# Order of DVE's work in the V stage: the fourth SwiGLU unit's products ahead of the statistics of tiles 10 and 11

## The chip, the cores and the metric

The kernel runs on one core of a Trainium2 chip. The metric is the device time of one execution in microseconds (us); the time of a kernel is the median of several executions. The engines are called PE (TensorE, matmuls), DVE (VectorE), ACT (ScalarE), POOL (GpSimd) and SP (SyncE, which here issues the DMAs). Each engine works through its own list of instructions in order, and waits where an instruction needs what another engine or a DMA has not yet finished.

## The reference

With x of 2048 tokens by 640 features (bf16), the kernel computes the sum of x, a linear attention and a SwiGLU block, both of them on the same layer norm of x:

```python
xn  = layernorm(x)                              # over 640 features, eps 1e-5
# A: linear attention with the hedgehog feature map, 32 heads of 20
q, k, v = split_heads(xn @ wqkv)
pq, pk  = q @ w_phi, k @ w_phi                  # per head, 20 x 20
phi_q = concat(softmax(pq), softmax(-pq));  phi_k = concat(softmax(pk), softmax(-pk))
kv = phi_k^T @ v;   z = sum over tokens of phi_k
A  = merge_heads((phi_q @ kv) / (phi_q . z + 1e-6)) @ wo
# B: SwiGLU with 1536 hidden features
B  = (silu(xn @ w1) * (xn @ w3)) @ w2
out = x + A + B
```

## The kernel before, in words

The 2048 tokens are 16 tiles of 128. The order of all instructions is written out by hand (`manual_schedule`): what stands earlier in the source stands earlier in the list of its engine, and the framework adds the waits and hands out the buffers. The stages are: an opening with the layer norm of the first tiles; the V stage, in which all tiles are normalized and transposed and V is computed; a stage over 16 tiles for phi_k and kv; and a stage over 16 tiles for phi_q, the quotient and the output. SwiGLU units are put in between as filling for PE.

In the V stage the steps of a tile t are these.

- `stats(t0, n)`: `ln_stats` on DVE for each tile (two BATCH_NORM_STATS2, L205, and an aggregate, L208), then on POOL, for the n tiles together, `ln_pow` (L216, L219) and `ln_newton` (L233 to L244), which make the reciprocal standard deviation `rstd`. For tiles 12 and 13 POOL adds `shift` (L246).
- `lx(t0, n)`: x is normalized in place, on DVE (L259), or for tiles 12 and 13 on ACT (L254), with `rstd` and the mean (or `shift`).
- `T(t, ...)`: the tile's transpose into `xnT`, for t of 4 and up a transposing DMA on SP's queue (L269). On the same queue, in the order written, stand `ldT` (L122), which loads blocks of the key and query weights transposed, and the plain loads (L109).
- `V(t)`: ten matmuls on PE into two PSUM banks (L295), and three copies by ACT into `vaug` (L308).
- `FB(d)`: the key weights' block d is multiplied by w_phi on PE (L377) with the masked weights `wphi`, which DVE makes once in `phi_blocks()` (L368), and ACT copies it into `wkphi` (L386).

A SwiGLU unit is split in two. `unit()` puts ten matmuls on PE (gate `gp` and up `up`, L393, one PSUM bank each) and the tanh on ACT (L401) where it stands. It returns a function, and where this is called (`g0()` to `g5()`), DVE does the products: L406 (from tanh and gate, which frees the gate's bank) and L409 (times up, which frees the up bank). So the source says apart when PE does a unit and when DVE does its products.

`V`, the units and later steps take their PSUM banks from one pool of six (`bank`); which bank a step gets depends on which were given back before it in the source.

The stage's end, after the lines of the change, is

```python
        V(9)
        g5 = unit()
        lx(13, 1)
        T(13)
        ldT(wkT, 1, 3)
        V(10)
        phi_blocks()
        g5()
        lx(14, 2)
        T(14, 15)
        ldT(wkT, 1, 4)
        V(11)
        ld_glu(512, F)
        ...
        V(12), FB(0), FB(1), V(13), FB(2), V(14), FB(3), V(15), FB(4)
```

Of the kernel before, what the change touches and what calls it, by code (L numbers as in the profile page):

```python
# [12 lines left out]
def kernel(  # L13
# [105 lines left out]
    with tc.manual_schedule():  # L119
# [81 lines left out]
        def ln_stats(t, between=None):  # L201
            xt = xin[:, (t // 4) % 3, t % 4, :]
            st = work.tile([P, 2, 6], f32, name="st")
            for i in range(2):
                nc.vector.bn_stats(out=st[:, i, :], in_=xt[:, i * HD : (i + 1) * HD])  # L205
                if i == 0 and between:
                    between()
            nc.vector.bn_aggr(out=mv[:, t, :], in_=st[:])  # L208
# [5 lines left out]
        def ln_pow(t, n):  # L214
            r = slice(t, t + n)
            nc.gpsimd.tensor_scalar(  # L216
                out=ve[:, r], in0=mv[:, r, 1], scalar1=EPS, scalar2=None, op0=ALU.add
            )
            nc.gpsimd.tensor_tensor(out=ry[:, r], in0=ve[:, r], in1=mhalf[:, 0:n], op=ALU.pow)  # L219
# [8 lines left out]
        def ln_newton(t, n):  # L228

            r = slice(t, t + n)  # L230
            eng = nc.gpsimd
            if n == 1:
                eng.tensor_scalar(  # L233
                    out=rstd[:, r], in0=ry[:, r], scalar1=ve[:, r], scalar2=ry[:, r],
                    op0=ALU.mult, op1=ALU.mult,
                )
            else:
                eng.tensor_mul(out=rstd[:, r], in0=ry[:, r], in1=ry[:, r])
                eng.tensor_mul(out=rstd[:, r], in0=rstd[:, r], in1=ve[:, r])
            eng.tensor_scalar(  # L240
                out=rstd[:, r], in0=rstd[:, r], scalar1=-0.5, scalar2=1.5,
                op0=ALU.mult, op1=ALU.add,
            )
            eng.tensor_mul(out=rstd[:, r], in0=rstd[:, r], in1=ry[:, r])  # L244
            if t in BY_ACT:
                eng.tensor_scalar(  # L246
                    out=shift[:, r], in0=mv[:, r, 0], scalar1=rstd[:, r], scalar2=-1.0,
                    op0=ALU.mult, op1=ALU.mult,
                )
# [138 lines left out]
        def glu_unit(sc, fi):  # L388

            gp, up = bank("gp"), bank("up")  # L390
            for ps, w in ((gp, w1), (up, w3)):
                for c in range(KD):
                    nc.tensor.matmul(  # L393
                        ps[:],
                        w[:, c, fi * P : (fi + 1) * P],
                        xnT[:, c, sc * 512 : (sc + 1) * 512],
                        start=(c == 0),
                        stop=(c == KD - 1),
                    )
            th = work.tile([P, 512], f32, name="th")  # L400
            nc.scalar.activation(out=th[:], in_=gp[:], func=AF.Tanh, scale=0.5)  # L401
            return lambda: glu_product(sc, fi, gp, up, th)
# [175 lines left out]
        def stats(t0, n):  # L578
            for t in range(t0, t0 + n):
                ln_stats(t)  # L580
            ln_pow(t0, n)
            ln_newton(t0, n)

        def lx(t0, n):
            if t0 < BY_DMA:
                nc.vector.reciprocal(out=rstd[:, t0 : t0 + n], in_=ry[:, t0 : t0 + n])
            for t in range(t0, t0 + n):
                ln_x(t)
# [13 lines left out]
        def unit():  # L602
            return glu_unit(*glu.pop(0))
# [52 lines left out]
        g3 = unit()  # L656
# [3 lines left out]
        ldT(wkT, 1, 2)  # L660
        V(4)
        V(5)
        stats(10, 2)
        g3()
        V(6)
        V(7)
        stats(12, 1)
        g4 = unit()
        lx(10, 2)
        T(10, 11)  # L670
        stats(13, 1)
        V(8)
        g4()
        stats(14, 2)
        lx(12, 1)
        T(12)
        V(9)
        g5 = unit()
        lx(13, 1)
# [123 lines left out]
```

## Time and profile before

| | |
|---|---|
| median of 3 runs | 270.49 us (270.46 to 270.83) |
| the profiled execution | 270.34 us |
| its span, first to last instruction | 268.5 us |
| granted PE clock, mean | 1.000 |
| busy: PE, DVE, ACT, POOL | 263.7, 188.7, 111.6, 95.3 us |
| 21.90 to 44.45 us: PE, DVE, ACT, POOL busy | 22.32, 13.89, 14.48, 8.91 of 22.55 us |

Times in the profile are counted from the first instruction. The stretch from 21.90 to 44.45 us is the V stage from V(4) on. A line of the timeline has the start, the length, the engine, the source line, the operation with its result and inputs, and how many like instructions are merged; in brackets, how long the engine stood idle before it and what ended that. "SPq" is the issue of a DMA on SP's queue.

### The profile page before, as it was taken

The page shows a single profiled execution, that of the slowest core. Times are in us where ns is not written, and L with a number is a line of the kernel's source. Part 1 is how long each engine was busy: PE and PEld are TensorE (multiplying, and loading weights), DVE is VectorE, ACT ScalarE, POOL GpSimd, SP SyncE. Part 2 cuts the span into 40 slices and gives each one's busy share as a digit, 9 for nine tenths or more (in the row PEclk, how much of TensorE's full clock was granted, in tenths as well). Part 3 has the DMA queues.
Part 4 walks back from the last instruction along what each step waited for, and adds up shares of the span by engine and source line. Part 5 has one row for each costly group of instructions (what it writes and reads, how often), then busy time and mean ns, then how long its engine had stood idle before and what let it go on. Part 6 is the DMA issues. An engine that isn't in the chain of part 4 may idle for free.

```text
span 268.5 us, 5276 instructions
## 1 busy us (share of the span) xinstructions
PE 263.7 (98%) x1990; PEld 166.2 (62%) x1990; DVE 188.7 (70%) x348; ACT 111.6 (42%) x342; POOL 95.3 (35%) x99
## 2 busy tenths in 40 slices
PE   8999999999999999999999999999999999999995
PEld 7646567555555555555555445677777777777773
DVE  4899940887766677777777888966766777776341
ACT  3854568544555554346556545422222222221000
POOL 5054730354433333334444321233344444433000
DMA  6996647970000000000000854345555555565831
GB/s 215 351 221 123 77 99 222 270 193 4 0 0 2 1 2 0 0 4 0 0 2 0 242 162 98 81 122 137 125 143 142 129 129 127 132 147 131 155 98 55
DMA packets 63101, 27.81 MB, mean 104 GB/s; under 512 B 50144, under 2 KB 61792, under 8 KB 63072
## 3 DMA queue, kind: packets, MB, share of 16 engines
q1 hardware_dynamic: 63072, 27.43, 42.1%
q8 instruction: 17, 0.28, 0.4%
q14 instruction: 12, 0.10, 0.1%
HBM read 12.81 MB, written 2.62 MB: 57 GB/s over the span
## 4 chain that ended last, share of the span: by engine, by line
PE 89%; DVE 4%; POOL 2%; DMA 2%; issue 1%; SPq 1%; ACT 1%; DVEq 0%
PE acc L517 28%; PE gp L393 18%; PE up L393 18%; PE pq L295 8%; PE pk L295 8%; PE pv L295 5%; PE pr L454 2%; PE pkv L419 2%; DMA reg_w<-in_A_wqkv_dram 2%; DVE st L205 1%; PE pf L377 1%; SPq L109 1%; DVE reg_h L259 1%; POOL ry L219 1%; DVE gs L406 0%
## 5 line engine op out<-in xcount | busy, mean ns | idle before, releaser
L359 POOL TENSOR_TENSOR phi<-phi,rk 128x1320 bf16<-128x1320 bf16 x32 | 77.2, 2413 | 134.1 <-DVE rk L358 99.2
L356 DVE TENSOR_REDUCE sk<-phi 128x66 f32<-128x1320 bf16 x32 | 48.9, 1528 | 41.8 <-ACT phi L322 40.8
L393 PEld LDWEIGHTS <-w 128*128 128x128 bf16 x480 | 45.5, 98 | 50.6
L393 PE MATMUL up<-xnT,w 128*128 128x512 bf16 x240 | 59.6, 379 | 0.0
L393 PE MATMUL gp<-xnT,w 128*128 128x512 bf16 x240 | 59.6, 378 | 0.0
L295 PEld LDWEIGHTS <-xnT 128*128 128x128 bf16 x480 | 45.4, 98 | 21.6 <-issue 1.0
L517 PE MATMUL acc<-reg_v,reg_h 128*128 128x320 bf16 (+2 forms) x384 | 54.9, 299 | 0.0
L322 ACT ACTIVATE phi<-pq 128x360 bf16<-128x360 f32 (+2 forms) x96 | 24.8, 364 | 58.0 <-issue 44.1
L517 PEld LDWEIGHTS <-reg_h 128*128 128x128 bf16 x384 | 37.3, 98 | 14.4
L401 ACT ACTIVATE th<-gp 128x512 f32<-128x512 f32 x48 | 28.9, 602 | 32.9 <-PE gp L393 32.9
L409 DVE SCALAR_TENSOR_TENSOR reg_h<-gs,up 128x512 bf16<-128x512 bf16 x48 | 33.0, 688 | 4.9
L322 ACT ACTIVATE phi<-pk 128x360 bf16<-128x360 f32 (+2 forms) x96 | 24.8, 364 | 24.1 <-PE pk L295 24.1
L406 DVE SCALAR_TENSOR_TENSOR gs<-th,gp 128x512 bf16<-128x512 f32 x48 | 31.5, 657 | 0.3 <-ACT th L401 0.3
L526 DVE TENSOR_TENSOR res<-acc,xr 128x320 bf16<-128x320 f32 (+2 forms) x32 | 14.3, 487 | 20.0 <-PE acc L517 20.0
L295 PE MATMUL pk<-wkphi,xnT 128*128 128x360 bf16 (+1 forms) x160 | 24.5, 299 | 0.0
L517 PE MATMUL acc<-reg_w,reg_v 128*128 128x320 bf16 (+2 forms) x160 | 24.5, 299 | 0.0
L295 PE MATMUL pq<-wqphi,xnT 128*128 128x360 bf16 (+1 forms) x160 | 24.3, 299 | 0.0
L295 PE MATMUL pv<-reg_w,xnT 128*128 128x360 bf16 (+1 forms) x160 | 23.7, 299 | 0.4 <-DVE gs L406 0.2
L358 DVE RECIPROCAL rk<-sk 128x66 f32<-128x66 f32 x32 | 18.1, 567 | 3.5 <-DVE sk L356 0.5
L517 PEld LDWEIGHTS <-reg_v 128*128 128x128 bf16 x160 | 15.7, 98 | 6.1
L308 ACT CAST reg_v<-pv 128x360 bf16<-128x360 f32 (+2 forms) x48 | 13.2, 353 | 7.7 <-PE pv L295 7.6
L205 DVE BATCH_NORM_STATS2 st<-reg_h 128x6 f32<-128x320 bf16 x32 | 13.8, 471 | 2.8 <-DMA reg_h<-in_A_x_dram 2.8
(66 smaller groups left out, 132.8 us busy)
## 6 DMA issues: line engine op xcount, KB each, us to landing
w<-in_B_w_dram SPq DMA_DIRECT2D x2, 1280.0 KB, 8.6
xr<-in_A_x_dram SPq DMA_DIRECT2D x16, 160.0 KB, 2.5
out_dram<-res SPq DMA_DIRECT2D x15, 160.0 KB, 1.8
reg_h<-in_A_x_dram SPq DMA_DIRECT2D x7, 320.0 KB, 5.4
reg_v<-in_B_w_dram SPq DMA_DIRECT2D x4, 480.0 KB, 5.4
w<-in_B_w_dram SPq DMA_DIRECT2D x4, 320.0 KB, 6.5
reg_w<-in_A_wqkv_dram SPq DMA_DIRECT2D x2, 320.0 KB, 4.2
reg_w<-in_A_wo_dram SPq DMA_DIRECT2D x1, 480.0 KB, 4.7
```

The costliest lines, as they stand in the source:

```text
L205: nc.vector.bn_stats(out=st[:, i, :], in_=xt[:, i * HD : (i + 1) * HD])
L295: nc.tensor.matmul(ps[i][:, 0 : b - a], xnT[:, c, cols], w[:, c, a:b], start=(c == 0), stop=(c == KD - 1), skip_group_check=True,)
L322: nc.scalar.activation(out=dst[:, c0 : c0 + n, g, 0:k], in_=p.rearrange("p (c f) -> p c f", c=n), func=AF.Exp, scale=1.0 - 2.0 * g,)
L356: nc.vector.reduce_sum(out=sk[:], in_=rows, axis=AX.X)
L358: nc.vector.reciprocal(out=rk[:], in_=sk[:])
L359: nc.gpsimd.tensor_mul(out=rows, in0=rows, in1=rk[:, :, :, None].to_broadcast([P, 2 * NCH, 3, Dh]))
L393: nc.tensor.matmul(ps[:], w[:, c, fi * P : (fi + 1) * P], xnT[:, c, sc * 512 : (sc + 1) * 512], start=(c == 0), stop=(c == KD - 1),)
L401: nc.scalar.activation(out=th[:], in_=gp[:], func=AF.Tanh, scale=0.5)
L406: nc.vector.scalar_tensor_tensor(out=gs[:], in0=th[:], scalar=1.0, in1=gp[:], op0=ALU.add, op1=ALU.mult)
L409: nc.vector.scalar_tensor_tensor(out=hT[:, 4 * sc : 4 * sc + 4, fi, :], in0=gs[:].rearrange("p (t s) -> p t s", t=4), scalar=0.5, in1=up[: ...
L517: nc.tensor.matmul(ps[:, 0 : b - a], rows[j][0], rows[j][1][:, a:b], start=(j == 0), stop=(j == len(rows) - 1),)
L526: nc.vector.tensor_tensor(out=res[:, a:b], in0=ps[:, 0 : b - a], in1=xr[:, a:b], op=ALU.add)
```

## The change

DVE does the fourth unit's products (`g3()`) ahead of the statistics of tiles 10 and 11. The fifth unit's products (`g4()`) come ahead of the statistics of tile 13, and those of tiles 14 and 15 come after the transpose of tile 12 is written. The statement `g4 = unit()` trades places with `stats(12, 1)`, which changes no engine's order. The instructions on PE, ACT, POOL and SP keep their order; the PSUM banks of the V steps and units from V(6) on are other ones.

```diff
         V(4)
         V(5)
+        g3()
         stats(10, 2)
-        g3()
         V(6)
         V(7)
+        g4 = unit()
         stats(12, 1)
-        g4 = unit()
         lx(10, 2)
         T(10, 11)
-        stats(13, 1)
         V(8)
         g4()
-        stats(14, 2)
+        stats(13, 1)
         lx(12, 1)
         T(12)
+        stats(14, 2)
         V(9)
         g5 = unit()
         lx(13, 1)
```

## The prediction

> **What bounds the kernel now.** I read the page first, then TensorE's gaps, then each engine's timeline from 20 to 46 us, where the moved lines run. The page's busy shares and its chain of work:
>
> ```profile
> PE 263.7 (98%) x1990; PEld 166.2 (62%) x1990; DVE 188.7 (70%) x348; ACT 111.6 (42%) x342; POOL 95.3 (35%) x99
> ...
> PE 89%; DVE 4%; POOL 2%; DMA 2%; issue 1%; SPq 1%; ACT 1%; DVEq 0%
> ```
>
> TensorE (PE) is busy 98% of the span and carries 89% of the chain, at a granted clock of 1.00 throughout. So DVE time is worth nothing by itself: an edit counts only by the time in which PE stands still. Between 21.9 and 44.45 us (the V stage after its SwiGLU opening) the timeline of PE shows one stall:
>
> ```profile
> 24.32 1.95 PE L295 MATMUL pv<-reg_w,xnT 128*128 128x360 bf16 x13
> 26.49 0.28 PE L295 MATMUL pv<-reg_w,xnT 128*128 128x280 bf16 x1 [0.23 <-DVE gs L406]
> ```
>
> This is the second matmul of V(7). Singly, its predecessor starts at 25.95 and the usual distance of such a pair is 0.15 us; here it is 0.54. The stall is therefore 0.39 us, not the 0.23 shown (ends of matmuls are modelled). The bank that V(7) takes was read by the fourth unit's first product (`g3()`, L406). DVE shows why that is late:
>
> ```profile
> 23.77 0.88 DVE L205 BATCH_NORM_STATS2 st<-reg_h 128x6 f32<-128x320 bf16 x2
> 24.69 0.21 DVE L208 BATCH_NORM_AGGREGATE mv<-st 128x2 f32<-128x12 f32 x1
> 24.81 0.83 DVE L205 BATCH_NORM_STATS2 st<-reg_h 128x6 f32<-128x320 bf16 x2
> 25.68 0.21 DVE L208 BATCH_NORM_AGGREGATE mv<-st 128x2 f32<-128x12 f32 x1
> 25.81 0.63 DVE L406 SCALAR_TENSOR_TENSOR gs<-th,gp 128x512 bf16<-128x512 f32 x1
> ```
>
> The statistics of tiles 10 and 11 stand ahead of it, though its tanh was done at 21.6. It ends at 26.44; V(7) goes on 0.05 later.
>
> Downstream of the statistics is a long line: aggregate on DVE, a chain of small operations on POOL, the normalization `lx` (DVE; ACT for tiles 12 and 13), the transposing DMA on SP's queue, then V(t) on PE. POOL for tile 13 and the start for 14 and 15, then SP:
>
> ```profile
> 30.80 0.22 POOL L216 TENSOR_SCALAR ve<-mv 128x1 f32<-128x1 f32 x1
> ...
> 32.47 0.19 POOL L244 TENSOR_TENSOR rstd<-rstd,ry 128x1 f32<-128x1 f32 x1
> 32.77 0.26 POOL L246 TENSOR_SCALAR shift<-mv,rstd 128x1 f32<-128x1 f32 x1
> 33.44 0.86 POOL L216 TENSOR_SCALAR ve<-mv 128x2 f32<-128x2 f32 x1 [0.41 <-DVE mv L208]
> ```
>
> ```profile
> 34.40 0.91 ACT L254 ACTIVATE reg_h<-reg_h,shift,rstd 128x640 bf16<-128x640 bf16 x1
> ```
>
> ```profile
> 35.34 1.20 SPq L269 DMA_TRANSPOSE xnT<-reg_h  x1
> 36.59 1.27 SPq L122 DMA_TRANSPOSE reg_w<-in_A_wqkv_dram  x1
> 37.95 2.55 SPq L269 DMA_TRANSPOSE xnT<-reg_h  x2
> 40.55 1.27 SPq L122 DMA_TRANSPOSE reg_w<-in_A_wqkv_dram  x1
> ```
>
> From T(13) on, SP issues back to back: T(13), weight block 3, T(14), T(15), weight block 4. So T(14) follows T(13) by 2.61 us whatever its own input does. The landing records put T(14)'s end at 40.39; PE loads V(14)'s first weights at 41.05. Slack: 0.66 us. Others: T(13) 37.72 against 39.38 (1.65), T(15) 41.65 against 42.72 (1.07), block 4 43.42 against 44.02 (0.60). These slacks are what the change spends.
>
> **The change, part by part.** Two units' products move: `g3()` ahead of the statistics of 10 and 11, `g4()` ahead of those of 13, and 14/15 go behind T(12) in the order written. No instruction is added; PE, ACT, POOL and SP keep their order. The banks of the later units are permuted, so waits must be redone.
>
> *The stall goes.* Each pair of products takes 1.34 us of DVE (25.81 to 27.15), each tile's statistics 0.99 to 1.04. `g3()` now starts at 23.77 and its two outputs are out at 24.40 and 25.20. In the new assignment V(6) and V(7) take its banks, at 24.59 and 25.95; with the 0.05 seen above both are in time, V(6) by 0.13. So PE is 0.39 us early from V(7) on: -0.39. V(14)'s load would come at 40.66, block 4's at 43.63, and the slacks shrink to 0.27 and 0.21.
>
> *Tiles 10 and 11.* Their statistics end 1.34 later, at 27.23, and POOL's two-tile chain takes 2.13 (25.98 to 28.10 before), so its result is there at 29.45. DVE is free for `lx(10)` at 28.19, as before, and now waits to 29.48: 1.29 us of new idle time. Queued behind it are `g4()`, statistics 13, 14, 15, the masked weights (L368) and the rest. T(10) starts at 29.91 instead of 28.61, lands by 33.6 even if it keeps its odd 2.55 us issue, and V(10) loads at 34.1: hidden. T(11) and T(12) are hidden likewise, with over half a us each. Without this cover each would cost its lateness.
>
> *Tile 13, the step that decides.* With `lx(10)` at 29.48, `g4()` starts at 30.15 and statistics 13 at 31.49, ending at 32.61 (was 29.98). POOL starts its chain 0.09 later, at 32.70; by the rows above L244 runs from 34.38 to 34.57 and L246 from 34.68 to 34.94. On DVE, statistics 14 and 15 follow at once (2.03 us, as 31.24 to 33.27), and L368 runs from 34.57 to 35.50 (0.94 us in the trace). L246 falls into L368.
>
> What does that cost? Two rows bound it. Before, POOL's L216 at 33.44 fell into L368 (33.27 to 34.21): it took 0.86 us instead of 0.22 and ended 0.09 after L368. Another L216, at 15.26, ran beside DVE's L259 (15.21 to 15.66) in 0.22: nothing. I take the first, the same DVE instruction. L246 then ends at 35.59; ACT's `lx(13)` runs 0.05 to 0.96 later, to 36.55; T(13) starts at 36.58, 1.24 later than before. By the other bound `lx(13)` ends at 35.89 and T(13) starts at 35.92, 0.58 later.
>
> The Trainium skill, "SBUF — State Buffer", section "Who interferes with whom", says that a DVE instruction with two SBUF inputs and a GpSimd one that reads SBUF exclude each other, the later fully waiting. By it the sum is the +0.68 below rather than +0.02. The 0.86 row agrees; the page counts some `tensor_scalar` forms too, which the row at 15.26 does not show.
>
> *PE at the end of the stage.* With 1.24 T(14) lands at 41.63. The load follows a landing by 0.04 (an early V matmul: landing 7.74, start 7.78) and the matmul by 0.12, so V(14) starts at 41.79, against 41.11 before: +0.68. From there PE runs as before: T(15) lands at 42.89, block 4 at 44.66 against a load at 44.70, just in time. The wait of 0.2 us at 45.75 for ACT's last copy of the fused weights follows PE and stays. V(10)'s copies on ACT wait behind `lx(13)` for 0.3 us; their banks are wanted again at 38.7, over 1 us after the copies. DVE's products of unit five (L406, L409) end about 36.9, before V(12) wants that second bank at 37.2. Tiles 14 and 15: POOL's chain ends near 37.8, `lx(14)` by 38.3, before SP reaches T(14) at 39.19. The later issues on SP (w1/w3's rest, wq's blocks) move by 1.2 us; the wq blocks are first used at 69.7 and were all issued by 55.6.
>
> Sum: -0.39 and then +1.07 of new stall at V(14), net +0.68. After 46 us PE is fully fed and clocked, so the shift is carried to the end. Against the profiled execution's own 270.34 us (span 268.5) this is 271.02; the median of the runs shown is 270.49, 0.15 above it, so the forecast is 271.17.
>
> **The rivals.**
> 1. *L246 is not held* (it slips in ahead of L368, or the lock is not there for it). T(13) is 0.58 late, V(14) starts at 41.13: +0.02, 270.5. For: the 15.26 row, and L246 misses L368's start by only 0.11 us. Against: the 0.86 row.
> 2. *L244 is held too*: it ends within 0.01 of L368's start. L246 then ends at 35.96, T(13) is 1.61 late: +1.05, 271.55. Against: POOL would have started 0.19 earlier.
> 3. *The removed stall stands: faster.* If T(13) is not over 0.17 us late (issued by 35.5), V(14) never waits: -0.39, 270.1. It decides by T(13)'s issue; between 0.17 and 0.56 late the gain melts to nothing. For: PE's own row shows the stall going. Against: the 2.13 us POOL chain, which the new order puts between the statistics and `lx(10)` with nothing else for DVE to do.
> 4. A wait I placed as just hidden (V(6)'s bank, block 4) costs some tenths on top: within the upper end.
>
> **How the numbers follow.** Forecast 0.55, rival 1 0.20, rival 2 0.10, rival 3 0.10, the rest 0.05. The break-even is a lateness of T(13) of 0.56 us; 0.2% of this kernel is 0.54 us, about what its measurement can tell from no change, and is reached at 1.10 late, near the forecast's 1.24. So of the forecast's 0.55 I put 0.07 inside 0.2%. Slower: 0.48 + 0.10 + 0.04 = 0.62. Same: 0.07 + 0.18 = 0.25. Faster: rival 3 and a part of rival 1, 0.13. The range runs from rival 1 less its 0.2 us of play, 270.3, to rival 2 with 0.15 more, 271.7; rival 3 and the tail above stay out.
>
> **What would show it.** Right: no wait of V(7) on L406; `lx(10)` waiting about 1.3 us for POOL's L244; an L246 of some 0.9 us beside L368; T(13) issued near 36.6; PE waiting about 1 us for the landing of T(14) near 41 us; equal distances after 46 us. Wrong: L246 at 0.26 us, T(13) before 35.9, or no wait of V(14); or a stall of PE anywhere else in the stage.

## The result and the profile after

| | before | changed |
|---|---|---|
| median of 14 runs | 270.48 us (269.98 to 271.16) | 271.24 us (270.69 to 271.92) |
| ratio, 95% interval | | 1.0023 [1.0014, 1.0032] |
| span of the profiled execution | 268.5 us | 269.0 us |

The kernel is slower by 0.23%. The two spans differ by 0.47 us only, because the profiled executions reach V(4) at different times (21.88 and 21.59 us): the opening varies from one execution to the next. So the traces are compared from V(4)'s first matmul on. To the second phi_k step it takes 48.17 - 21.88 = 26.30 us before and 48.64 - 21.59 = 27.05 us after: +0.76 with the unrounded times. From there to the last instruction both take 220.35 us. In the traces, the whole difference is made between V(4) and the first phi_k step.

The chain of work that ended last now has a transpose's DMA (L269) and POOL's `shift` (L246) in it:

```profile
PE 93%; ACT 1%; POOL 1%; DMA 1%; DVE 1%; issue 1%; SPq 1%
PE acc L517 27%; PE up L393 19%; PE gp L393 18%; PE pq L295 8%; PE pk L295 8%; PE pv L295 6%; PE pr L454 2%; PE pkv L419 2%; PE idle L184 2%; DMA xnT<-reg_h 1%; PE pf L377 1%; ACT reg_v L308 1%; PE pst L273 0%; SPq L122 0%; POOL shift L246 0%
```

PE's timeline. First FB(2) (`pf`) and V(14) (`pv`) in the kernel before, for comparison:

```profile
40.79 0.48 PE L377 MATMUL pf<-wphi,reg_w 128*128 128x140 bf16 x6
41.11 1.52 PE L295 MATMUL pv<-reg_w,xnT 128*128 128x360 bf16 x10
```

Now the changed kernel, V(6) and V(7) first, then FB(2), V(14) and FB(3) at the stage's end:

```profile
24.03 3.15 PE L295 MATMUL pv<-reg_w,xnT 128*128 128x360 bf16 x22
...
40.24 0.48 PE L377 MATMUL pf<-wphi,reg_w 128*128 128x140 bf16 x6
41.56 1.53 PE L295 MATMUL pv<-reg_w,xnT 128*128 128x360 bf16 x10 [0.85 <-DMA xnT<-reg_h]
42.93 0.48 PE L377 MATMUL pf<-wphi,reg_w 128*128 128x140 bf16 x6
```

The bracket on L406 is gone from the row of V(6) and V(7), and V(14) now waits for its transpose. Its first matmul starts 1.32 us after FB(2)'s, where it was 0.32 before: 1.00 us of wait.

DVE, with the new idle time ahead of `lx(10)`, and then the masked weights:

```profile
23.49 0.68 DVE L406 SCALAR_TENSOR_TENSOR gs<-th,gp 128x512 bf16<-128x512 f32 x1
...
29.24 0.80 DVE L259 TENSOR_SCALAR reg_h<-reg_h,mv,rstd 128x640 bf16<-128x640 bf16 x2 [1.26 <-POOL rstd L244]
...
34.37 0.94 DVE L368 TENSOR_TENSOR wphi<-wps,mask 128x800 bf16<-128x800 bf16 x1
```

POOL's chain for tile 13 beside it, ACT's `lx(13)`, and SP's queue from T(13) on:

```profile
34.23 0.19 POOL L244 TENSOR_TENSOR rstd<-rstd,ry 128x1 f32<-128x1 f32 x1
34.53 0.91 POOL L246 TENSOR_SCALAR shift<-mv,rstd 128x1 f32<-128x1 f32 x1
```

```profile
35.47 0.92 ACT L254 ACTIVATE reg_h<-reg_h,shift,rstd 128x640 bf16<-128x640 bf16 x1 [1.64 <-POOL shift L246]
```

```profile
36.42 1.20 SPq L269 DMA_TRANSPOSE xnT<-reg_h  x1
37.67 1.27 SPq L122 DMA_TRANSPOSE reg_w<-in_A_wqkv_dram  x1
39.03 2.55 SPq L269 DMA_TRANSPOSE xnT<-reg_h  x2
```

L246 takes 0.91 us instead of 0.26 and ends 0.13 after L368 (which ends at 35.31). T(13) is issued 14.83 us after V(4)'s start instead of 13.47, and T(14) follows it by 2.61, as before.

### The profile page after: what moved, and what is told of

It reads as the page before. It is cut to its first block, busy times and chain, and to the rows that moved or that the text cites. A ratio compares the mean times of both kernels' runs of the same rounds, so it can differ in the third digit from the quotient of the medians.

```text
span 269.0 us, 5259 instructions
## 1 busy us (share of the span) xinstructions
PE 263.0 (98%) x1973; PEld 166.5 (62%) x1990; DVE 188.7 (70%) x348; ACT 111.6 (41%) x342; POOL 95.2 (35%) x99
## 4 chain that ended last, share of the span: by engine, by line
PE 93%; ACT 1%; POOL 1%; DMA 1%; DVE 1%; issue 1%; SPq 1%
PE acc L517 27%; PE up L393 19%; PE gp L393 18%; PE pq L295 8%; PE pk L295 8%; PE pv L295 6%; PE pr L454 2%; PE pkv L419 2%; PE idle L184 2%; DMA xnT<-reg_h 1%; PE pf L377 1%; ACT reg_v L308 1%; PE pst L273 0%; SPq L122 0%; POOL shift L246 0%
## 5 line engine op out<-in xcount | busy, mean ns | idle before, releaser
L393 PE MATMUL gp<-xnT,w 128*128 128x512 bf16 x226 | 58.5, 378 | 0.6
L406 DVE SCALAR_TENSOR_TENSOR gs<-th,gp 128x512 bf16<-128x512 f32 x48 | 31.6, 658 | 0.0
```

Source lines behind the costliest of these rows:

```text
L393: nc.tensor.matmul(ps[:], w[:, c, fi * P : (fi + 1) * P], xnT[:, c, sc * 512 : (sc + 1) * 512], start=(c == 0), stop=(c == KD - 1),)
L406: nc.vector.scalar_tensor_tensor(out=gs[:], in0=th[:], scalar=1.0, in1=gp[:], op0=ALU.add, op1=ALU.mult)
```

## The experiments

Every ratio is to the kernel before. "PE shift" is the change of the time from V(4)'s first matmul to the second phi_k step's, in that kernel's profiled execution; unlike the ratio it is one execution's, but it does not hold the variation of the opening. "T(13)" is its issue counted from V(4)'s start. From the second phi_k step to the last instruction these executions took 220.34 or 220.35 us, but 220.45 in experiment 6, 220.62 in 8 and 220.81 in the first execution of 7; only for the last is a reason given below.

| kernel | ratio, 95% interval | PE shift, us | T(13), us | last L246, us |
|---|---|---|---|---|
| before | 1 | 0 | 13.47 | 0.26 |
| changed | 1.0023 [1.0014, 1.0032] | +0.76 | 14.83 | 0.91 |
| 1: fourth unit's products alone | 0.9986 [0.9977, 0.9996] | -0.39 | 13.22 | 0.26 |
| 2: masked weights later | 1.0005 [0.9995, 1.0014] | +0.11 | 14.18 | 0.26 |
| 3: later half alone | 1.0012 [1.0003, 1.0020] | +0.10 | 14.20 | 0.91 |
| 4: tile 13 on DVE | 1.0004 [0.9995, 1.0014] | -0.06 | 13.35 | none for 13 |
| 5: masked weights twice | 1.0032 [1.0021, 1.0043] | +0.77 | 14.84 | 0.91 |
| 6: weight block 3 first | 0.9995 [0.9985, 1.0004] | -0.18 | 14.88 | 0.90 |
| 7: 1 and FB(4)'s copies first | 0.9989 [0.9979, 1.0000] | -0.57 | 13.29 | 0.26 |
| 8: masked weights split | 1.0024 [1.0010, 1.0037] | +0.70 | 14.82 | 0.90 |
| 1 again | 0.9988 [0.9977, 0.9999] | -0.37 | 13.28 | 0.26 |
| 7 again | 0.9982 [0.9968, 0.9996] | -0.54 | 13.28 | 0.26 |

**1. The fourth unit's products alone.**

```diff
 # against the kernel before
+        g3()
         stats(10, 2)
-        g3()
```

> Only the fourth unit's products are moved ahead of the statistics of 10 and 11; the rest of the order is that of before. Main theory (the time comes from tile 13's chain: statistics 13 late, then POOL's L246 held behind DVE's L368): lx(10) still waits about 1.3 us for POOL, but statistics 13 run right behind it, POOL's chain for 13 ends near 34.1, well ahead of L368, T(13) is issued no later than before (about 35.1), V(14) does not wait, and the removed stall stands: 0.39 us faster than before, ratio 0.9986. Rival (the new idle time of DVE ahead of lx(10), or the other PSUM banks, cost the time by themselves): both are here as well, so slower than before by some 0.7 us, ratio 1.0025.

Measured: 0.9986, PE shift -0.39. DVE idles as long ahead of `lx(10)` as in the changed kernel, and the V steps' PSUM banks are the same ones, yet PE waits for neither. So the idle time and the banks by themselves are not what costs. Statistics 13 stand in front of the fifth unit's products here, and L246 is through before L368 begins; the next L216, for tiles 14 and 15, is held instead:

```profile
33.44 0.26 POOL L246 TENSOR_SCALAR shift<-mv,rstd 128x1 f32<-128x1 f32 x1
34.42 0.86 POOL L216 TENSOR_SCALAR ve<-mv 128x2 f32<-128x2 f32 x1 [0.71 <-DVE mv L208]
```

T(14) is issued 16.21 after V(4)'s start (16.08 before), because `lx(14)` is now what it waits for, and that is still in time. This half of the change alone is a gain, the whole 0.39 us of the stall.

**2. The masked weights behind the fifth unit's products.**

```diff
 # against the changed kernel
-        phi_blocks()
         g5()
+        phi_blocks()
```

> The changed kernel, with the masked weights (L368) after the fifth unit's products instead of ahead of them; nothing else. Main theory (L368 holds POOL's L246 by about 0.65 us, and T(13) and V(14) follow): L246 takes about 0.26 us again, T(13) is issued about 0.65 us earlier than in the changed kernel, PE's wait at V(14) falls by as much, and the kernel is about 0.1 us over before (ratio 1.0004). Rival (L246 is long for another reason, such as its place in POOL's list, or V(14) waits for another input): L246 stays at 0.9 us or V(14)'s wait stays, ratio 1.0023.

Measured: 1.0005, PE shift +0.11, which is 0.65 less than in the changed kernel, as L246 is shorter by 0.65. L368 runs at 36.65 here, and the POOL instruction beside it is now the long one (L238 takes 0.19 elsewhere):

```profile
35.46 0.26 POOL L246 TENSOR_SCALAR shift<-mv,rstd 128x1 f32<-128x1 f32 x1
...
36.91 0.77 POOL L238 TENSOR_TENSOR rstd<-ry 128x2 f32<-128x2 f32 x1
```

```profile
41.84 1.53 PE L295 MATMUL pv<-reg_w,xnT 128*128 128x360 bf16 x10 [0.32 <-DMA xnT<-reg_h]
```

So L246 is long because of L368, and not because of its place. V(14), in the last row, starts 0.66 us earlier, counted from V(4), than in the changed kernel: what L246 lost came out there in full.

**3. The later half alone.**

```diff
 # against the kernel before
+        g4 = unit()
         stats(12, 1)
-        g4 = unit()
         lx(10, 2)
         T(10, 11)
-        stats(13, 1)
         V(8)
         g4()
-        stats(14, 2)
+        stats(13, 1)
         lx(12, 1)
         T(12)
+        stats(14, 2)
```

> Only the later half of the change: the fourth unit's products stay behind the statistics of 10 and 11, the fifth's come ahead of the statistics of 13, and those of 14 and 15 one place later. Main theory: V(7)'s stall of 0.39 us stays; lx(10) does not wait, statistics 13 end near 31.3, POOL's chain for 13 near 33.6, before ACT is free for lx(13), so T(13) is issued as before (35.3) and V(14) does not wait: no change, ratio 1.000. Rival (putting statistics 13 behind the fifth unit is enough to make tile 13 late): slower than before by 0.3 us or more.

Measured: 1.0012, PE shift +0.10; V(7)'s stall stays, T(13) is 0.74 late and L246 takes 0.91. My expectation had tile 13 on time and missed it: I had `g4()` start right behind `lx(10)`, but the tanh of that unit was not yet done.

```profile
28.53 0.75 DVE L259 TENSOR_SCALAR reg_h<-reg_h,mv,rstd 128x640 bf16<-128x640 bf16 x2
29.95 0.69 DVE L406 SCALAR_TENSOR_TENSOR gs<-th,gp 128x512 bf16<-128x512 f32 x1 [0.66 <-ACT th L401]
```

Before, statistics 13 filled this time. With 0.66 us of idle DVE the statistics of 13 slide far enough for L246 to fall into L368 again. V(14)'s slack of 0.66 us eats nearly all of T(13)'s 0.74, so the price is 0.1 us. That would be a ratio of 1.0004, which the interval holds only near its lower end, 1.0003.

**4. Tile 13 normalized on DVE.**

```diff
 # against the changed kernel
-    BY_ACT = (12, 13)
+    BY_ACT = (12,)
```

> The changed kernel, with tile 13 normalized on DVE instead of ACT, so that L246 for 13 does not exist and L259 waits for L244 alone. Main theory (the lateness of tile 13 comes through L246 and ACT): T(13) is issued near 35.0, about 1.5 us earlier than in the changed kernel, V(14) does not wait, and the kernel is 0.39 us faster than before (ratio 0.9986). Rival (V(14)'s wait hangs on the statistics 14 and 15 or on SP's queue alone): V(14) still waits about 0.8 us and the ratio stays near 1.002.

Measured: 1.0004, PE shift -0.06. T(13) is 1.48 us earlier than in the changed kernel and V(14) does not wait, as expected. But the gain is gone elsewhere: with `lx(13)` ahead of L368 on DVE, the fifth unit's second product ends 0.5 us later, and V(12) waits for the bank that it frees:

```profile
38.65 1.37 PE L295 MATMUL pv<-reg_w,xnT 128*128 128x280 bf16 x9 [0.17 <-DVE reg_h L409]
```

By starts the pair is 0.48 us apart instead of 0.15, so the wait is 0.33 us. I had not carried DVE's extra instruction on to the products behind it. L368 meets another POOL instruction here, in the chain for tiles 14 and 15 (L219 takes 0.71 elsewhere), and V(14) is still in time:

```profile
35.94 0.40 POOL L216 TENSOR_SCALAR ve<-mv 128x2 f32<-128x2 f32 x1
36.43 1.35 POOL L219 TENSOR_TENSOR ry<-ve,mhalf 128x2 f32<-128x2 f32 x1
```

**5. The masked weights twice.**

```diff
 # against the changed kernel
         phi_blocks()
+        phi_blocks()
         g5()
```

> The changed kernel, with the masked weights computed twice in a row (L368 twice, the same result). Main theory (POOL's L246 is held until L368 is done): L246 takes about 0.94 us more, 1.85 us, T(13) and T(14) are issued 0.94 us later, PE's waits up to V(14) grow by as much, ratio about 1.0063 to before. Rival (L246 has 0.9 us for another reason): T(13) stays where it is in the changed kernel; the fifth SwiGLU unit's products come 0.94 us later and PE waits about 0.7 us for them at V(12), but V(14)'s wait shrinks by that, ratio about 1.0028.

Measured: 1.0032, PE shift +0.77. T(13) stays where it was and the ratio is near the rival's 1.0028, but not for the rival's reason, which experiment 2 has ruled out. What fails is the main theory's step that POOL is held for the pair: L246 ends 0.13 after the first L368 (which ends at 35.73), and the next POOL instruction is held by the second:

```profile
34.95 0.91 POOL L246 TENSOR_SCALAR shift<-mv,rstd 128x1 f32<-128x1 f32 x1
35.94 0.90 POOL L216 TENSOR_SCALAR ve<-mv 128x2 f32<-128x2 f32 x1
```

```profile
34.79 1.97 DVE L368 TENSOR_TENSOR wphi<-wps,mask 128x800 bf16<-128x800 bf16 x2
```

The second L368 writes the same tile and starts 0.03 us after the first has ended; L246 is let go there. PE waits 0.22 us at V(12) for the delayed L406, and V(14)'s wait for T(14) swallows that.

**6. Weight block 3 ahead of T(13) on SP's queue.**

```diff
 # against the changed kernel
+        ldT(wkT, 1, 3)
         T(13)
-        ldT(wkT, 1, 3)
```

> The changed kernel, with the DMA of weight block 3 issued ahead of T(13) instead of behind it, in the time in which SP's queue waits for tile 13; DVE, POOL, ACT and PE keep their order. Main theory (V(14) waits for T(14), and T(14) is late because it stands behind T(13) and block 3 on SP's queue): L246 stays at 0.9 us and T(13) stays where it is, T(14) is issued 0.9 us earlier, right behind lx(14), V(14)'s wait falls from about 1.0 us to 0.2, ratio about 0.9998. Rival (V(14) waits for tile 14's own statistics and POOL chain): T(14) and V(14) stay, ratio 1.0025.

Measured: 0.9995, PE shift -0.18. L246 stays held and T(13) late, but T(14) is issued 16.63 after V(4)'s start instead of 17.45, and no wait of V(14) worth a bracket is left. SP's rows, with block 3 in the gap:

```profile
34.15 1.27 SPq L122 DMA_TRANSPOSE reg_w<-in_A_wqkv_dram  x1
36.82 4.27 SPq L269 DMA_TRANSPOSE xnT<-reg_h  x3
```

So V(14) waits for T(14), and T(14) is late because of what stands ahead of it on the queue. This alone, with the rest of the change kept, takes the loss away; whether a gain is left, the ratio's interval does not say.

**7. The first experiment's kernel, and ACT copies FB(4)'s result ahead of V(15)'s.**

```diff
 # against experiment 1: v_unit can run a step between its matmuls and its copies
-        def v_unit(t, cols=None, between=(KD, None)):
+        def v_unit(t, cols=None, between=(KD, None), late=None):
             ps = by_token(cols or tile_of(t), wv, "pv", CH, between)
+            if late:
+                late()
...
-        V(12), FB(0), FB(1), V(13), FB(2), V(14), FB(3), V(15), FB(4)
+        V(12), FB(0), FB(1), V(13), FB(2), V(14), FB(3), V(15, late=lambda: FB(4))
```

> The kernel of the first experiment (only the fourth unit's products moved), and in addition ACT copies FB(4)'s fused weights ahead of V(15)'s result instead of behind it; PE's order is the same. It should take away the last wait of PE in the stage, 0.21 us for ACT's L386 in the first phi_k step, on top of the 0.39 us: ratio about 0.9978 by the trace. If V(15)'s copies or their banks are wanted earlier than I see, the 0.21 comes back as another wait and the ratio stays at 0.9986.

Measured: 0.9989, PE shift -0.57. By the trace the last wait of the stage is gone, but from the second phi_k step to the end this execution took 220.81 us instead of 220.35. The last output's DMA landed 2.07 us after its issue there, and 1.54 us after it before, which is where the time went. Hence the repetition below.

**8. The masked weights split in two.**

```diff
 # against the changed kernel, in phi_blocks
-            nc.vector.tensor_mul(
-                out=wphi[:],
-                in0=wps[:, :, None, :].to_broadcast([P, KD, 8, Dh]),
-                in1=mask[:, :, :, None].to_broadcast([P, KD, 8, Dh]),
-            )
+            for c, n in ((0, 2), (2, 3)):
+                nc.vector.tensor_mul(
+                    out=wphi[:, c : c + n],
+                    in0=wps[:, c : c + n, None, :].to_broadcast([P, n, 8, Dh]),
+                    in1=mask[:, c : c + n, :, None].to_broadcast([P, n, 8, Dh]),
+                )
```

> The changed kernel, with L368 split into two instructions of 320 and 480 elements; the same result. Theory as it stands after the doubled L368 (POOL's L246 is held for the one DVE instruction that runs when it starts, and goes through before the next): L246 takes about 0.4 us instead of 0.91, T(13) is issued about 0.5 us earlier, V(14)'s wait shrinks by as much, about 0.25 us over before, ratio about 1.0009. Rival (DVE's two parts overlap and leave POOL no place between them): L246 stays at 0.9 us, ratio 1.0028 as in the changed kernel.

Measured: 1.0024, PE shift +0.70; L246 takes 0.90 as in the changed kernel. The second part starts 0.08 us before the first ends (34.39 to 34.83, 34.74 to 35.39), and POOL found no place between them:

```profile
34.39 1.00 DVE L369 TENSOR_TENSOR wphi<-wps,mask 128x320 bf16<-128x320 bf16 x2
```

```profile
34.54 0.90 POOL L246 TENSOR_SCALAR shift<-mv,rstd 128x1 f32<-128x1 f32 x1
```

**1 and 7 again, on one chip.**

> The first experiment again (only the fourth unit's products moved), beside the next kernel on the same chip: ratio 0.9986.

> The first experiment's kernel with FB(4)'s copies ahead of V(15)'s, again: its trace had PE 0.57 us early to the last weight load, but 0.4 us was lost in the wait for the last DMA at the end. If that was the one execution's chance, ratio about 0.9979 and a normal end; if it belongs to this kernel, about 0.9989 and the same wait at the end.

Measured: 0.9988 and 0.9982, PE shifts -0.37 and -0.54, both with 220.34 us to the end. The long end of the first one was that execution's own. The first phi_k step shows what the order of ACT's copies is worth, 1.72 us against 1.52. First the kernel of experiment 1 (its first execution), then that of 7 (its second):

```profile
43.66 1.72 PE L295 MATMUL pk<-wkphi,xnT 128*128 128x360 bf16 x10
```

```profile
44.35 1.52 PE L295 MATMUL pk<-wkphi,xnT 128*128 128x360 bf16 x10
```

Both versions beat the kernel before and the changed one: all four intervals end at or below 1. That 7 is faster than 1 is seen in the traces alone (0.18 and 0.17 us of PE shift); the intervals of the ratios overlap.

## Why the prediction was right

**The stall goes, 0.39 us.** Right: V(6) and V(7) run through, and experiment 1 has this term alone, -0.39 in the trace.

**`lx(10)` waits 1.29 us for POOL.** 1.26 measured. That T(10) to T(12) are hidden is right: PE runs from V(7) to V(12) without a wait. The odd 2.55 us issue of T(10) did not come back (1.20 us), which changed nothing.

**L246 falls into L368 and is held.** The bound chosen was the 0.86 us row of L216: L246 took 0.91. Experiment 2 parted the two bounds: without L368 beside it L246 takes 0.26, and 0.65 us of PE shift go with it. Rival 1 is out, and so is rival 2: L244 ran in 0.19 and ended at 34.42, just after L368 had begun.

What the prediction set against this, the row at 15.26, was read too widely. Two other stretches of the same trace show POOL held beside L259:

```profile
21.51 0.44 DVE L259 TENSOR_SCALAR reg_h<-reg_h,mv,rstd 128x640 bf16<-128x640 bf16 x1
21.61 0.77 POOL L219 TENSOR_TENSOR ry<-ve,mhalf 128x1 f32<-128x1 f32 x1
```

```profile
28.19 0.75 DVE L259 TENSOR_SCALAR reg_h<-reg_h,mv,rstd 128x640 bf16<-128x640 bf16 x2
28.36 0.30 POOL L216 TENSOR_SCALAR ve<-mv 128x1 f32<-128x1 f32 x1 [0.26 <-DVE mv L208]
```

The same two take 0.57 and 0.22 us at 31.10 and 30.80, and in experiment 4 an L216 took 0.40 beside L259. In these rows POOL started 0.09 to 0.17 us after L259, at 15.26 only 0.05. So that row was no sign that L246 would go free.

The Trainium skill, "SBUF — State Buffer", section "Who interferes with whom", has the ports that the two engines share go to one of them for its whole instruction, while the other waits. The traces agree in each case in which a POOL instruction began beside L368: 0.90 and 0.91 us for L246, 0.77 for L238, 0.86 and 0.90 for L216, 1.35 for L219.

**T(13), T(14), V(14).** T(13) was to be 1.24 us late and was 1.36; T(14) followed by 2.61 as said. The difference of 0.12 has two parts. By small slots on DVE, counted from V(4), `lx(10)` starts 0.05 later than worked out, `g4()` 0.1, statistics 13 0.14 (9.76 after V(4)'s start; predicted 31.49 - 21.88 = 9.61), and L368, after shorter statistics of 14 and 15, 0.09. And L246 ends 0.13 after L368 and not the 0.09 taken from L216's row. The net was to be +0.68 and is +0.76. V(13) also waits a little: 2.10 us from V(12)'s first matmul to V(13)'s instead of 1.99. The prediction missed this, though a stall elsewhere in the stage was one of its own signs of being wrong: T(13)'s slack of 1.65 just covered 1.24 of lateness and the 0.39 by which PE is early, and does not cover 1.36. This one costs nothing, since V(14) waits for T(14) anyway.

**Carried to the end.** Right to 0.01 us: 220.35 us from the second phi_k step to the last instruction in both.

**The rival of the other side** (the removed stall stands) did not come, by the step that it named: T(13) was over 0.17 us late. Experiments 1 and 6 show that it was near. Without the later half, or with one DMA earlier on SP's queue, the PE shift is -0.39 or -0.18 us.

**The halves don't add up.** Alone they shift PE by -0.39 and +0.10, together by +0.76, which the prediction did not ask about. Only together do the fifth unit's products follow `lx(10)`'s wait of 1.26 us and stand ahead of statistics 13, so that T(13) is 1.36 late; the halves alone had it 0.25 early and 0.74 late. And with the first half PE is 0.39 us early, so V(14) has that much less slack to cover it.

What the runs don't settle is the size beyond the trace: the ratio's interval, 0.38 to 0.87 us, holds the 0.76 but does not resolve the terms. These rest on one trace of each kernel and on the experiments that remove one of them.

## What to carry to other kernels

When the first of two queued pieces of work is put ahead, follow the other piece to its last reader: here a matmul stall of 0.39 us went, and tile 13's transpose came 1.36 us late, on a line (POOL, ACT, one in-order DMA queue, PE) with 0.66 us of slack at its end. Add up slacks at the end of such lines before moving their start, and subtract what the gain itself takes from them. And before calling a change of several moves bad, take it apart: the first move alone is 0.14% faster (0.12% when it was run again), the others alone cost little, and the loss comes from having both.

## What the runs showed of the hardware

- A POOL instruction that starts while DVE's two-input L368 runs is shown as a long busy instruction, not as a wait: 0.77 to 0.91 us instead of 0.19 to 0.26, ending 0.05 to 0.13 after L368 (and L219 1.35 instead of 0.71). It is worth looking for in the durations, since the views of waits do not name it. Beside L259 the same happens on a smaller scale (0.77 instead of 0.57, 0.30 and 0.40 instead of 0.22), but not where POOL started only 0.05 us behind it.
- Between two such DVE instructions POOL got in where the first had ended before the second started (0.03 us were enough in experiment 5), and did not where they overlapped (0.08 us in experiment 8); that is one execution of each. Splitting the long instruction in this way was no remedy; moving it was.
- The opening up to V(4) took between 21.47 and 22.98 us in the profiled executions, though its order is the same in all of these kernels. One execution's span therefore can't show a change of 0.3%, and the time between two fixed matmuls can: it came within 0.03 us of itself in the two kernels that were run again.
